# One product of two weight matrices in fp32 instead of split fp32r, and another rating of transfers in the planner

## The chip, the cores and the metric

The kernel runs on one core of one Trainium2 chip. The metric is the device time of one execution in microseconds (us); the kernel before was run three times, and its median counts.

## What is computed

Causal attention with a compressive memory, then two feed-forward blocks. The weights arrive as 8-byte floats (float64) and are converted on the chip.

```python
def _attn_ref(q, k, v, M_prev, z_prev, beta):      # B, H, S, D = 4, 8, 576, 64
    scores = scale * np.matmul(q, k.transpose(0, 1, 3, 2))
    ...                                            # causal mask, softmax
    local = np.matmul(a, v)
    q_p = phi(q)                                   # elu(q) + 1
    mem_out = einsum(q_p, M_prev) / (einsum(q_p, z_prev)[..., None] + 1e-06)
    g = 1.0 / (1.0 + np.exp(-beta))
    return g * mem_out + (1 - g) * local

def _moe_ref(x, w1, w2, w3, w_out):                # 2304 tokens, 512 wide, d_ff = 1024
    a = x @ w1
    b = x @ w2
    h = a * b @ w3
    return h @ w_out

def _moe2_ref(x, w_in, w_out):                     # d_ff = 2048
    h = x @ w_in
    g = h * np.tanh(softplus(h))
    return g @ w_out
```

## The kernel before

**The split.** A product of two fp32 matrices is mostly done as three fp32r products: each factor is split into a high part (a ScalarE cast to fp32r) and a low part (a VectorE subtraction of the high part from the value), and high x high, high x low and low x high are summed in PSUM (`HL`). The scores take two such products. The first twelve attention tasks (`T.f32`, `AVF=12`) multiply V with the exponentials, and M with PH, in plain fp32.

**w3 and w_out.** The first feed-forward block's last two factors are multiplied with each other once, ahead of everything that needs them: w3 @ w_out is 1024 x 512, computed as eight row blocks `f`. `load_wo(f)` brings a 128 x 512 block of w_out, `load_w3(f, hf)` a half of the transposed rows that belong to output block `f` (128 x 512), and `w3_mm(f, hf)` multiplies: for each of the eight 128-row blocks `c` of w_out three matmuls of 512 columns accumulate into one PSUM bank `w3p[f]`. After the second half the bank is split into wA buffers (L729 is the VectorE step), which ffn1 later uses as weights (`w3s`).

**Conversion.** `conv` loads a block of float64 (512 KB) into a raw buffer (`u`, `wE`, `wA`, or others), and builds an fp32 tile `c` from it: one ScalarE activation on the high words, one VectorE shift of the low words (L683), one VectorE shift-and-or that joins them (L685). `c` comes from the shared scratch tag `t`. `load_w` then splits `c` into a two-part fp32r tile: a cast (L337) and a subtraction (L333). Weights live in the tags `wA` (8 buffers), `wB` (8), `wD` (4), `wE` (4). w_out takes eight `wB`, each half block of w3 one `wD`. Later w1 and w2 go to `wE`, `wB` and `wD` (`fill_w12`), and the second feed-forward block's weights (`load_ffn2`) take whatever tags come free.

**Order.** Every operation is first recorded (`op`) with an engine, an estimated duration and the tiles that it reads and writes. `schedule` then simulates the engines with these estimates and fixes, for each engine, the order in which its instructions are issued; a buffer's next user waits until the last user of the buffer is done. Transfers are all issued by SyncE (SP), in the planner one after the other, each with the duration that `dma` states (250 bytes a ns, at least 500 ns), and behind it `LAT["sp"]` and `DMM`. TensorE's operations go by the order of recording, shifted by `GB` for the feed-forward work; the other engines go by the longest remaining chain. On the chip each engine runs its list in order, and waits where an input isn't there.

**The order of the work.** The loop over `heads` (two heads for each task; batch 0 is split into two halves of its rows) records for each step the scores of one head (`SC`), the AV product of the head before, the exponentials (`SE`), the memory product (`MEM`), and between them a share of the feed-forward work. In the first nine steps this share is w_out and w3: `start_w3` at step 0, `fill_w3` at the steps behind it, each with the two loads of block `f` and the product of block `f - 1`. w1 and w2 are loaded from step 6 on. After the eighth head the outputs X of batch 0's first half are there and ffn1 (`g<-x,wE` is its first product) begins. A task's output goes through transfers: the row sums (R) to memory `d`, back as `cp`, their reciprocals to memory again, and back broadcast as `Rr`, with which `mnl` is scaled and becomes `x`. ffn2 follows when all of ffn1 is done.

Of the kernel before, what the change touches and what calls it, by code (L numbers as in the profile page):

```python
# [8 lines left out]
F32 = mybir.dt.float32  # L9
F32R = mybir.dt.float32r  # L10
BF16 = mybir.dt.bfloat16
I32 = mybir.dt.int32
AF = mybir.ActivationFunctionType
ALU = mybir.AluOpType
P = 128
# [56 lines left out]
class Recorder:  # L72
# [9 lines left out]
    def op(self, eng, cost, fn, r=(), w=()):  # L82
        o = Op()
        o.eng, o.cost, o.fn, o.idx = eng, cost, fn, len(self.ops)
        o.deps, o.after, o.bufs, o.bias = set(), set(), [], self.bias
        for items, writing in ((r, False), (w, True)):
            for it in items:
                b, key = it if isinstance(it, tuple) else (it, None)
                if b not in o.bufs:
                    o.bufs.append(b)  # L90
                    if b.users:
                        o.after.add(b.users[0])
                    b.users.append(o)
                for k2, (ws, rs) in b.state.items():
                    if key is None or k2 is None or k2 == key:
                        o.deps.update(ws)
                        if writing:
                            o.deps.update(rs)
                if writing:
                    if key is None:  # L100
                        b.state.clear()
                    b.state[key] = ([o], [])
                else:
                    b.state.setdefault(key, ([], []))[1].append(o)
        o.deps.discard(o)
        o.after.discard(o)
        o.after -= o.deps
        self.ops.append(o)
        return o
# [136 lines left out]
def t_act(n, psum=False):  # L246
    return 0.833 * n + (51 if psum else 88)


def t_dve(n, fast=False):  # L250
    return (0.52 if fast else 1.042) * n + 68
# [6 lines left out]
def t_mm(n, m=128):  # L258
    return max(n * 0.433 + 7, m * 0.834)
# [3 lines left out]
def kernel(  # L263
# [15 lines left out]
    nc = tc.nc  # L279
    B, H, D, S = q.shape  # L280
    NT, DM = out.shape
    moe_w1, moe_w2, moe_w3, moe_w_out, moe2_w_in, moe2_w_out = (
        w.bitcast(I32) for w in (moe_w1, moe_w2, moe_w3, moe_w_out, moe2_w_in, moe2_w_out)
    )
# [12 lines left out]
    M1 = FF1 // P  # L297
    M2 = FF2 // P
    scale = 1.0 / float(D) ** 0.5

    rec = Recorder()
    op = rec.op
# [14 lines left out]
    def buf(tag, shape, dtype=F32):  # L317
        pool = wp if tag[0] == "w" else sp_
        return Buf(pool, shape, dtype, tag, BUFS[tag])
# [3 lines left out]
    def gbuf():  # L323
        return Buf(psG, [P, 512], F32, "g", 8)

    def dma(dst, src, nbytes, r=(), w=()):
        op("sp", max(500, nbytes / 250.0), lambda: nc.sync.dma_start(out=dst(), in_=src()), r, w)

    def mm(o, lhsT, rhs, start, stop):
        nc.tensor.matmul(out=o, lhsT=lhsT, rhs=rhs, start=start, stop=stop)  # L330
# [4 lines left out]
    def act(n, o, i, r, w, psum=False, func=AF.Copy, **kw):  # L335
        if func == AF.Copy:
            op("act", t_act(n, psum), lambda: nc.scalar.copy(out=o(), in_=i()), r, w)  # L337
        else:
            op("act", t_act(n, psum), lambda: nc.scalar.activation(out=o(), in_=i(), func=func, **kw), r, w)  # L339

    def lo(n, o, a, h, r, w, eng="dve"):
        e = nc.vector if eng == "dve" else nc.gpsimd
        op(eng, t_dve(n) if eng == "dve" else t_pool(n), lambda: sub(e, o(), a(), h().bitcast(F32)), r, w)
# [97 lines left out]
    def load_vm(T):  # L441
        j = T.nj
        n = 2 * j * DV
        if T.f32:
            M = T.M = buf("M", [P, VZ])
            dma(lambda: Vf.tile[:, T.i % 2, 0:j], lambda: v[T.b, T.p, :, 0:j], 512 * n, w=[(Vf, T.i % 2)])
            dma(lambda: M.tile, lambda: mz[T.b, T.p], 66560, w=[M])
            return
        raw = buf("vr", [P, VZ + 2 * NJ * DV])
        mr = lambda: raw.tile[:, 0:VZ]  # L450
        vr = lambda: raw.tile[:, VZ:VZ + n].rearrange("p (j t d) -> p j t d", t=2, d=DV)
        dma(vr, lambda: v[T.b, T.p, :, 0:j], 512 * n, w=[(raw, 0)])
        dma(mr, lambda: mz[T.b, T.p], 66560, w=[(raw, 1)])

        M = T.M = buf("M", [P, 2 * VZ], F32R)
        act(VZ, lambda: M.tile[:, 0:VZ], mr, [(raw, 1)], [(M, 0)])
        for a, b, c in ((0, P, VZ + 2), (P, VZ, VZ)):
            lo(b - a, lambda a=a, b=b, c=c: M.tile[:, c:c + b - a], lambda a=a, b=b: mr()[:, a:b], lambda a=a, b=b: M.tile[:, a:b], [(raw, 1), (M, 0)], [(M, 1)])
        act(n, lambda: Vb.tile[:, 0, 0:j], vr, [(raw, 0)], [(Vb, 0)])
        lo(n, lambda: Vb.tile[:, 1, 0:j], vr, lambda: Vb.tile[:, 0, 0:j], [(raw, 0), (Vb, 0)], [(Vb, 1)])  # L460
# [209 lines left out]

    def conv(src, rawb, c=None):
        raw = rawb()
        c = c or buf("t", [P, 512])
        flat = lambda: raw.tile.rearrange("p n w -> p (n w)")
        dma(flat, lambda: src, 524288, w=[raw])
        hw = lambda: raw.tile[:, :, 1]
        lw = lambda: raw.tile[:, :, 0]
        cv = lambda: c.tile  # L680
        ci = lambda: c.tile.bitcast(I32)
        act(512, cv, lambda: hw().bitcast(F32), [(raw, 1)], [c], False, AF.Prelu, scale=2.0 ** -111, alpha=-(2.0 ** 32))
        op("dve", t_dve(512, True), lambda: nc.vector.tensor_scalar(out=lw(), in0=lw(), scalar1=29, scalar2=None, op0=ALU.logical_shift_right),  # L683
           r=[(raw, 0)], w=[(raw, 0)])
        op("dve", t_dve(512), lambda: nc.vector.scalar_tensor_tensor(out=ci(), in0=ci(), scalar=3, in1=lw(), op0=ALU.logical_shift_left, op1=ALU.bitwise_or),  # L685
           r=[(raw, 0), c], w=[c])
        return c, cv

    def load_w(dst, src, m, tag, rawb, eng="dve"):
        c, cv = conv(src[m * P:(m + 1) * P, :], rawb)  # L690
        t = buf(tag, [P, 2, 512], F32R)
        act(512, lambda: t.tile[:, 0], cv, [c], [(t, 0)])
        lo(512, lambda: t.tile[:, 1], cv, lambda: t.tile[:, 0], [c, (t, 0)], [(t, 1)], eng)
        dst[m] = t
# [5 lines left out]
    w1s, w2s, w3s, wo, w3p, w3t = {}, {}, {}, {}, {}, {}  # L700

    def raw_u():
        return buf("u", [P, 512, 2], I32)

    def load_wo(f):
        load_w(wo, moe_w_out, f, "wB", lambda: buf("wA", [P, 512, 2], I32))

    def load_w3(f, hf):
        load_w(w3t, moe_w3, 2 * f + hf, "wD", lambda: buf("u" if hf or f > 5 else "wE", [P, 512, 2], I32))

    def w3_mm(f, hf):
        if hf == 0:
            w3p[f] = gbuf()
        ps = w3p[f]
        for c in range(4 * hf, 4 * hf + 4):

            def f2(c=c, t=w3t[2 * f + hf]):
                cs = slice((c - 4 * hf) * P, (c - 4 * hf + 1) * P)
                mm(ps.tile, t.tile[:, 0, cs], wo[c].tile[:, 0], c == 0, False)
                mm(ps.tile, t.tile[:, 0, cs], wo[c].tile[:, 1], False, False)  # L720
                mm(ps.tile, t.tile[:, 1, cs], wo[c].tile[:, 0], False, c == M1 - 1)

            t = w3t[2 * f + hf]
            op("pe", 3 * t_mm(512), f2, r=[(t, 0), (t, 1), (wo[c], 0), (wo[c], 1)], w=[ps])
        if hf == 0:
            return
        t = buf("wA", [P, 2, 512], F32R)
        act(512, lambda: t.tile[:, 0], lambda: ps.tile, [ps], [(t, 0)], True, AF.Identity, scale=2.0 ** -16)
        op("dve", t_dve(512), lambda: nc.vector.scalar_tensor_tensor(  # L729
            out=t.tile[:, 1], in0=ps.tile, scalar=2.0 ** -16, in1=t.tile[:, 0].bitcast(F32), op0=ALU.mult, op1=ALU.subtract),  # L730
           r=[ps, (t, 0)], w=[(t, 1)])
        w3s[f] = t
# [144 lines left out]
    def fill_w3(f):  # L877
        if f < M1:
            for hf in range(2):
                load_w3(f, hf)  # L880
        if f > CFG["W3G"]:
            w3_mm(f - 1, 0)
            w3_mm(f - 1, 1)

    def start_w3(hf):
        for f in range(4 * hf, 4 * hf + 4):
            load_wo(f)
        for f in range(CFG["W3G"]):
            load_w3(f, hf)
            w3_mm(f, hf)  # L890
# [15 lines left out]
    for i in range(NH_ + 1):  # L906
        if i < NH_:
            T, t = heads[i]
# [61 lines left out]
    for c in range(len(CH)):  # L970
        t0, n = CH[c]
        acc = []
        for t in range(n // P):
            x = gbuf()
# [69 lines left out]
```

## Time and profile before

| | |
|---|---|
| time, median of 3 runs | 989.56 us (988.12 to 990.38) |
| the profiled execution | 990.06 us, of which the span 988.3 us |
| TensorE busy | 948.4 us, 96% |
| VectorE busy | 742.1 us, 75% |
| ScalarE busy | 620.8 us, 63% |
| GpSimd busy | 82.6 us, 8% |
| moved by DMA | 96.63 MB, mean 98 GB/s |

The span runs from the first instruction to the last; the execution's time includes what lies around it. Matmuls are pipelined, so the time from one start to the next says what one costs, and a single record's duration is longer than that. PE is TensorE, PEld its weight loads, DVE VectorE, ACT ScalarE, POOL GpSimd, SP SyncE. The granted clock is a share of 2.4 GHz.

### The profile page before, as it was taken

To read this page: it belongs to the slowest core of one execution; us is meant where nothing else is said; L and a number is where in the kernel's file an instruction comes from. 1 tells how busy PE (TensorE), PEld (TensorE's weight loads), DVE (VectorE), ACT (ScalarE), POOL (GpSimd) and SP (SyncE) were. 2 spreads that over 40 slices of the span, in tenths; PEclk is the share of its full clock that TensorE was granted. 3 is DMA by queue.
4 is the path that set the end of the run, shared out by engine and by line. 5 is a ranking of instruction groups with operands and counts; after the bars stand their busy time and mean duration, and the time that the engine had idled before them with its cause. 6 is when DMAs were issued, how large, how long until landed. Compare 5 with 4: busy or idle time off the path is not lost.

```text
span 988.3 us, 15417 instructions
## 1 busy us (share of the span) xinstructions
PE 948.4 (96%) x5504; PEld 827.4 (84%) x5504; DVE 742.1 (75%) x1667; ACT 620.8 (63%) x1264; POOL 82.6 (8%) x70
## 2 busy tenths in 40 slices
PE   5897898999999999999999999999999999999998
PEld 3475796768999999999999998888888888998997
DVE  7899899999999898988562779665554756566663
ACT  5666587778988777866452667545444644555553
POOL 1111002221221111211000000000000000000000
PEclk7798799999999999999999999999999999999999
DMA  9436766643343332312471570011002000100000
GB/s 353 153 115 214 239 194 185 184 137 112 117 142 105 111 121 65 103 45 61 112 230 63 161 254 6 1 43 43 0 1 80 1 1 17 59 1 17 33 0 33
DMA packets 48317, 96.63 MB, mean 98 GB/s; under 512 B 11024, under 2 KB 23344, under 8 KB 48240
## 3 DMA queue, kind: packets, MB, share of 16 engines
q1 hardware_dynamic: 48240, 95.64, 30.7%
q8 instruction: 43, 0.70, 0.3%
q14 instruction: 34, 0.28, 0.1%
HBM read 85.85 MB, written 9.77 MB: 97 GB/s over the span
## 4 chain that ended last, share of the span: by engine, by line
PE 74%; DVE 15%; ACT 6%; issue 3%; DMA 2%; POOL 0%; SPq 0%; DVEq 0%; ACTq 0%; POOLq 0%
PE g L330 74%; DVE t L347 3%; DVE QK L333 3%; DVE e L347 2%; DVE t L685 1%; DVE mnl L347 1%; ACT t L339 1%; ACT e L339 1%; DVE g L560 1%; DVE u L333 1%; ACT mnl L337 1%; ACT t L337 1%; DVE wD L333 1%; DMA x2d<-t 0%; ACT QK L337 0%
## 5 line engine op out<-in xcount | busy, mean ns | idle before, releaser
L330 PE MATMUL g<-u,wA 128*128 128x288 f32 (+2 forms) x1008 | 163.0, 314 | 0.1
L330 PEld LDWEIGHTS g<-u,wA 128*128 128x128 f32 x1008 | 147.4, 188 | 8.9 <-DVE u L333 0.6
L347 DVE TENSOR_TENSOR t<-g,t 128x320 f32<-128x320 f32 (+6 forms) x344 | 122.5, 381 | 22.9 <-PE g L330 12.4
L580 POOL PARTITION_ALL_REDUCE t<-t x64 | 81.9, 1280 | 380.1 <-DVE t L347 310.7
L330 PE MATMUL g<-x,wB 128*128 128x288 f32 x768 | 111.0, 298 | 0.0
L330 PEld LDWEIGHTS g<-x,wB 128*128 128x128 f32 x768 | 104.9, 188 | 1.6 <-DVE t L347 0.7
L339 ACT ACTIVATE x<-x,two 128x512 f32<-128x512 f32 (+1 forms) x80 | 54.3, 681 | 68.9 <-DVE x L827 68.9
L330 PE MATMUL g<-e,V 128*65 128x320 f32 (+12 forms) x576 | 91.9, 306 | 4.6 <-ACT e L339 3.9
L339 ACT ACTIVATE x<-g 128x512 f32<-128x512 f32 (+1 forms) x98 | 55.0, 561 | 63.3 <-PE g L330 61.9
L330 PEld LDWEIGHTS g<-e,V 128*65 128x65 f32 (+1 forms) x576 | 67.2, 138 | 22.8 <-ACT e L339 6.6
L830 DVE SCALAR_TENSOR_TENSOR x<-g,x 128x512 f32<-128x512 f32 (+1 forms) x80 | 50.9, 638 | 42.0 <-ACT x L339 41.6
L330 PE MATMUL g<-QK 128*128 128x320 f32 (+7 forms) x464 | 72.7, 299 | 8.0 <-DVE QK L333 5.7
L330 PEld LDWEIGHTS g<-QK 128*128 128x128 f32 x464 | 64.9, 196 | 16.5 <-DVE QK L333 8.6
L337 ACT CAST x<-x 128x512 fp32r<-128x512 f32 (+1 forms) x80 | 46.1, 577 | 51.6 <-DVE x L347 51.4
L826 DVE TENSOR_SCALAR x<-x 128x512 f32<-128x512 f32 (+1 forms) x80 | 31.8, 398 | 61.7 <-ACT x L339 60.0
L330 PE MATMUL g<-wB,wD 128*128 128x512 f32 x192 | 58.7, 454 | 17.3 <-ACT wD L337 14.4
L333 DVE TENSOR_TENSOR t<-x 128x512 fp32r<-128x512 f32 (+1 forms) x80 | 50.9, 637 | 30.9 <-ACT x L337 29.6
L330 PEld LDWEIGHTS g<-wB,wD 128*128 128x128 f32 x192 | 39.3, 215 | 32.3 <-ACT wD L337 15.9
L333 DVE TENSOR_TENSOR QK<-ld,QK 64x640 fp32r<-64x640 f32 (+1 forms) x80 | 60.2, 753 | 2.8 <-ACT QK L337 1.3
L330 PE MATMUL g<-x,wE 128*128 128x288 f32 x384 | 55.5, 299 | 2.5 <-DVE e L347 1.9
L330 PE MATMUL g<-x,wD 128*128 128x288 f32 x384 | 57.0, 297 | 0.5 <-ACT t L339 0.5
L337 ACT COPY t<-g 128x288 f32<-128x288 f32 (+2 forms) x96 | 36.4, 393 | 32.4 <-PE g L330 26.3
(145 smaller groups left out, 1882.2 us busy)
## 6 DMA issues: line engine op xcount, KB each, us to landing
ld<-in_qk_dram SPq DMA_DIRECT2D x24, 608.0 KB
u<-in_moe_w_dram SPq DMA_DIRECT2D x26, 512.0 KB
Rr<-d SPq DMA_DIRECT2D x24, 288.0 KB
mnl<-in_moe_w_out_dram SPq DMA_DIRECT2D x11, 512.0 KB
mnl<-in_moe_w_in_dram SPq DMA_DIRECT2D x11, 512.0 KB
x2d<-t SPq DMA_DIRECT2D x16, 288.0 KB
out_dram<-x SPq DMA_DIRECT2D x18, 256.0 KB
wA<-in_moe_w_out_dram SPq DMA_DIRECT2D x8, 512.0 KB
```

The lines of the kernel that those rows point to most:

```text
L330: nc.tensor.matmul(out=o, lhsT=lhsT, rhs=rhs, start=start, stop=stop)
L333: eng.tensor_tensor(out=o, in0=a, in1=b, op=ALU.subtract)
L337: op("act", t_act(n, psum), lambda: nc.scalar.copy(out=o(), in_=i()), r, w)
L339: op("act", t_act(n, psum), lambda: nc.scalar.activation(out=o(), in_=i(), func=func, **kw), r, w)
L347: op(eng, t_dve(n) if eng == "dve" else t_pool(n), lambda: e.tensor_tensor(out=o(), in0=a(), in1=b(), op=alu), r, w)
L560: nc.vector.tensor_tensor(out=o, in0=o, in1=mv, op=ALU.add)
L580: op("pool", 430 + 2.6 * (b - a), lambda mv=mv: nc.gpsimd.partition_all_reduce(mv(), mv(), P, bass_isa.ReduceOp.max), r=[(m, x)], w=[(m, x)])
L685: op("dve", t_dve(512), lambda: nc.vector.scalar_tensor_tensor(out=ci(), in0=ci(), scalar=3, in1=lw(), op0=ALU.logical_shift_left, op1=ALU ...
L826: op("dve", t_dve(n, True), lambda: nc.vector.tensor_scalar(out=w_(), in0=u(), scalar1=E20, scalar2=2.0, op0=ALU.min, op1=ALU.add), r=[ub_ ...
L830: op("dve", t_dve(n), lambda: nc.vector.scalar_tensor_tensor(out=u(), in0=hv(), scalar=2.0 ** -8, in1=u(), op0=ALU.mult, op1=ALU.mult), r= ...
```

## The change

`conv` gets a parameter `part`: the fp32 value can be written into one part of a tile that the caller gives. `load_wo` and `load_w3` no longer split: they convert straight into fp32 tiles of two parts, two blocks of w_out to a `wB` tile, both halves of a block of w3 to a `wD` tile. `w3_mm` issues one fp32 matmul in place of three fp32r matmuls. The dependencies name the part. The planner's estimate for a transfer goes from 250 to 340 bytes a ns, for all transfers of the kernel, and that for a product of w3_mm to the fp32 rate.

```diff
--- before.py
+++ after.py
@@ -324,7 +324,7 @@
         return Buf(psG, [P, 512], F32, "g", 8)
 
     def dma(dst, src, nbytes, r=(), w=()):
-        op("sp", max(500, nbytes / 250.0), lambda: nc.sync.dma_start(out=dst(), in_=src()), r, w)
+        op("sp", max(500, nbytes / 340.0), lambda: nc.sync.dma_start(out=dst(), in_=src()), r, w)
 
     def mm(o, lhsT, rhs, start, stop):
         nc.tensor.matmul(out=o, lhsT=lhsT, rhs=rhs, start=start, stop=stop)
@@ -670,20 +670,21 @@
 
 
 
-    def conv(src, rawb, c=None):
+    def conv(src, rawb, c=None, part=None):
         raw = rawb()
         c = c or buf("t", [P, 512])
+        ck = (c, part)
         flat = lambda: raw.tile.rearrange("p n w -> p (n w)")
         dma(flat, lambda: src, 524288, w=[raw])
         hw = lambda: raw.tile[:, :, 1]
         lw = lambda: raw.tile[:, :, 0]
-        cv = lambda: c.tile
-        ci = lambda: c.tile.bitcast(I32)
-        act(512, cv, lambda: hw().bitcast(F32), [(raw, 1)], [c], False, AF.Prelu, scale=2.0 ** -111, alpha=-(2.0 ** 32))
+        cv = (lambda: c.tile) if part is None else (lambda: c.tile[:, part])
+        ci = lambda: cv().bitcast(I32)
+        act(512, cv, lambda: hw().bitcast(F32), [(raw, 1)], [ck], False, AF.Prelu, scale=2.0 ** -111, alpha=-(2.0 ** 32))
         op("dve", t_dve(512, True), lambda: nc.vector.tensor_scalar(out=lw(), in0=lw(), scalar1=29, scalar2=None, op0=ALU.logical_shift_right),
            r=[(raw, 0)], w=[(raw, 0)])
         op("dve", t_dve(512), lambda: nc.vector.scalar_tensor_tensor(out=ci(), in0=ci(), scalar=3, in1=lw(), op0=ALU.logical_shift_left, op1=ALU.bitwise_or),
-           r=[(raw, 0), c], w=[c])
+           r=[(raw, 0), ck], w=[ck])
         return c, cv
 
     def load_w(dst, src, m, tag, rawb, eng="dve"):
@@ -702,26 +703,28 @@
     def raw_u():
         return buf("u", [P, 512, 2], I32)
 
+
     def load_wo(f):
-        load_w(wo, moe_w_out, f, "wB", lambda: buf("wA", [P, 512, 2], I32))
+        if f % 2 == 0:
+            wo[f] = wo[f + 1] = buf("wB", [P, 2, 512])
+        conv(moe_w_out[f * P:(f + 1) * P, :], lambda: buf("wA", [P, 512, 2], I32), wo[f], f % 2)
 
     def load_w3(f, hf):
-        load_w(w3t, moe_w3, 2 * f + hf, "wD", lambda: buf("u" if hf or f > 5 else "wE", [P, 512, 2], I32))
+        if hf == 0:
+            w3t[f] = buf("wD", [P, 2, 512])
+        x = 2 * f + hf
+        conv(moe_w3[x * P:(x + 1) * P, :], lambda: buf("u" if hf or f > 5 else "wE", [P, 512, 2], I32), w3t[f], hf)
 
     def w3_mm(f, hf):
         if hf == 0:
             w3p[f] = gbuf()
-        ps = w3p[f]
+        ps, t = w3p[f], w3t[f]
         for c in range(4 * hf, 4 * hf + 4):
 
-            def f2(c=c, t=w3t[2 * f + hf]):
-                cs = slice((c - 4 * hf) * P, (c - 4 * hf + 1) * P)
-                mm(ps.tile, t.tile[:, 0, cs], wo[c].tile[:, 0], c == 0, False)
-                mm(ps.tile, t.tile[:, 0, cs], wo[c].tile[:, 1], False, False)
-                mm(ps.tile, t.tile[:, 1, cs], wo[c].tile[:, 0], False, c == M1 - 1)
-
-            t = w3t[2 * f + hf]
-            op("pe", 3 * t_mm(512), f2, r=[(t, 0), (t, 1), (wo[c], 0), (wo[c], 1)], w=[ps])
+            def f2(c=c, t=t):
+                mm(ps.tile, t.tile[:, hf, (c - 4 * hf) * P:(c - 4 * hf + 1) * P], wo[c].tile[:, c % 2], c == 0, c == M1 - 1)
+
+            op("pe", 2 * 0.833 * 512 + 4, f2, r=[(t, hf), (wo[c], c % 2)], w=[ps])
         if hf == 0:
             return
         t = buf("wA", [P, 2, 512], F32R)
```

## Rows read from the trace of the kernel before

**Rows 1.** The profile's page: TensorE's line of the busy times, and the granted clock over 40 equal slices of the span, in tenths.

```profile
PE 948.4 (96%) x5504; PEld 827.4 (84%) x5504; DVE 742.1 (75%) x1667; ACT 620.8 (63%) x1264; POOL 82.6 (8%) x70
...
PEclk7798799999999999999999999999999999999999
```

**Rows 2.** Windows over the whole span: the stretch in us, its length, the busy time of each engine with its instructions, TensorE's mean granted clock, the busy share of the DMA engines, GB/s.

```profile
5.00:15.00 10.00, 5.75 (x17) 3.73 (x18) 7.84 (x23) 5.86 (x12) 1.42 (x2) 0.94 1.02 404
...
95.00:103.60 8.60, 2.38 (x4) 0.59 (x4) 6.42 (x13) 4.68 (x10) 0.00 (x0) 0.54 0.93 278
...
113.00:150.00 37.00, 37.00 (x263) 34.39 (x263) 35.41 (x87) 29.87 (x67) 3.17 (x3) 1.00 0.62 199
150.00:250.00 100.00, 92.27 (x569) 72.18 (x568) 94.47 (x264) 77.89 (x174) 25.52 (x21) 1.00 0.50 147
250.00:300.00 50.00, 48.64 (x365) 46.12 (x364) 49.18 (x123) 44.33 (x99) 10.83 (x8) 1.00 0.43 128
...
400.00:988.00 588.00, 584.04 (x3217) 518.03 (x3216) 377.03 (x730) 319.08 (x608) 12.76 (x10) 1.00 0.18 57
```

**Rows 3.** The same view, with the first 113 us cut in three. The columns are those of PE, PEld, DVE, ACT and POOL, then the clock, the DMA share and GB/s.

```profile
0.00:37.00 37.00, 22.59 (x60) 13.04 (x61) 29.93 (x82) 22.96 (x43) 4.58 (x9) 0.78 0.72 272
37.00:83.00 46.00, 44.71 (x204) 32.50 (x204) 39.42 (x100) 30.20 (x64) 6.72 (x5) 0.96 0.51 161
83.00:113.00 30.00, 19.57 (x68) 14.08 (x67) 25.01 (x56) 18.17 (x37) 1.65 (x1) 0.72 0.75 236
```

**Rows 4.** The view of waits, from 0 to 113 us: who waited for whom, us in total, times, the longest.

```profile
PE g L330 <- ACT wD L337: 14.4, 5, 5.5
...
ACT wB L337 <- DVE t L685: 7.4, 7, 1.5
```

**Rows 5.** The timeline of TensorE: start in us, us until the end of the last of the group, and in brackets the idle time before it with what ended it. g<-wB,wD is the product of w3 and w_out, g<-x,wE the first of ffn1.

```profile
63.71 7.78 PE L330 MATMUL g<-wB,wD 128*128 128x512 f32 x33
71.33 1.14 PE L330 MATMUL g<-QK 128*128 128x288 f32 x6
...
103.65 8.40 PE L330 MATMUL g<-wB,wD 128*128 128x512 f32 x24 [5.49 <-ACT wD L337]
...
113.12 1.75 PE L330 MATMUL g<-x,wE 128*128 128x288 f32 x12
```

**Rows 6.** VectorE: two rows of the groups by line with the shapes apart, from 0 to 113 us (busy us, mean ns of one, idle before), and two of its timeline, one subtraction and what starts next.

```profile
L333 DVE TENSOR_TENSOR wD<-t,wD 128x512 fp32r<-128x512 f32 x16 | 11.5, 716 | 2.9 <-ACT wD L337 2.9
...
L333 DVE TENSOR_TENSOR wB<-t,wB 128x512 fp32r<-128x512 f32 x9 | 6.2, 690 | 1.6 <-ACT wB L337 1.6
...
45.12 0.68 DVE L333 TENSOR_TENSOR wD<-t,wD 128x512 fp32r<-128x512 f32 x1
45.72 0.78 DVE L347 TENSOR_TENSOR e<-g,t 128x288 f32<-128x288 f32 x3
```

**Rows 7.** The instructions on the tiles of wB over the whole span: ScalarE's casts (shortest, median and longest in ns, first and last start in us).

```profile
L337 ACT CAST wB<-t x24: 602/620/625, 11.6 to 569.2; 128x512 fp32r<-128x512 f32 x24
```

**Rows 8.** Products in plain fp32: the matmuls on the tile M over the whole span with their forms (those with 2 output rows are issued by the fp32 tasks alone), and lines of TensorE's timeline.

```profile
L330 PE MATMUL g<-PH,M x144: 289/299/847, 6.8 to 455.1; 128*128 128x288 f32 x80, 128*2 128x288 f32 x32, 128*4 128x288 f32 x32
...
165.92 0.65 PE L330 MATMUL g<-PH,M 128*128 128x288 f32 x2
166.40 1.25 PE L330 MATMUL g<-e,V 128*65 128x288 f32 x6
...
181.03 1.23 PE L330 MATMUL g<-PH,M 128*128 128x288 f32 x4
182.18 1.05 PE L330 MATMUL g<-u,wA 128*128 128x288 f32 x6
```

**Rows 9.** The waits of SyncE's queue, which issues the transfers, from 20 to 65 us.

```profile
SPq L327 <- DVE cp L653: 12.6, 1, 12.6
SPq L327 <- DVE PH L498: 12.0, 1, 12.0
```

**Rows 10.** Timelines of TensorE, SyncE and VectorE: the output of the fourth task from its last AV product to x, and (the first two lines) one transfer of Rr of an earlier task with the VectorE step that uses it.

```profile
75.16 1.25 SPq L327 DMA_DIRECT2D Rr<-d  x2
...
79.67 0.75 DVE L347 TENSOR_TENSOR mnl<-mnl,Rr 128x576 f32<-128x576 f32 x1
...
82.66 1.01 PE L330 MATMUL g<-e,V 128*65 128x288 f32 x6
...
84.68 0.52 SPq L327 DMA_DIRECT2D d<-R  x1
...
86.79 0.33 SPq L327 DMA_DIRECT2D cp<-d  x1
...
92.10 0.23 DVE L653 TENSOR_SCALAR cp<-cp,eps 128x9 f32<-128x9 f32 x1
...
93.76 0.33 SPq L327 DMA_DIRECT2D d<-cp  x1
...
96.16 1.23 SPq L327 DMA_DIRECT2D Rr<-d  x2
...
104.84 0.75 DVE L347 TENSOR_TENSOR mnl<-mnl,Rr 128x576 f32<-128x576 f32 x1
...
107.56 0.46 DVE L333 TENSOR_TENSOR x<-mnl,x 128x288 fp32r<-128x288 f32 x1
```

## The prediction

> **What bounds the kernel now.** I read the page's busy shares first: TensorE is busy 96% of the span and its granted clock is full except in some of the first five slices [rows 1]. That says where to look, not what is to be had. So next the windows. From 113 us on TensorE is nearly always busy: all of 113 to 150, 92.27 of 100 us in 150 to 250, 48.64 of 50, and 584.04 of 588 us after 400. VectorE is full beside it until 300 us (35.41 of 37, 94.47 of 100, 49.18 of 50) [rows 2]. Before 113 us, the stretch in which w3 and w_out are converted and multiplied, TensorE is busy 22.59 of 37, 44.71 of 46 and 19.57 of 30 us, at a granted clock of 0.78, 0.96 and 0.72 [rows 3]. Busy time times clock is 17.6 + 42.9 + 14.1 = 74.6 us of work at full clock in 113 us. The other 38.4 us are 26.1 us of idle time and 12.3 us lost to the clock, which stands at 0.54 in the emptiest piece [rows 2]; a 0.54 is nearly all at the lower level, 1.2 GHz. The loss is at both ends of the stretch, not in its middle.
>
> The waits say who causes it: TensorE waits 14.4 us for the ScalarE cast of w3 into wD, and ScalarE's cast into wB waits 7.4 us for the VectorE step before it [rows 4]. The timeline of TensorE shows the last wait at its place: the product of the last block of w3 starts at 103.65 us after 5.49 us idle, and at 113.12 us the first product of ffn1 follows it [rows 5]. So in the first stretch the conversion of weights decides at its ends, TensorE in its middle.
>
> **Part 1: casts and subtractions go.** Eight blocks of w_out and sixteen of w3 each lose one ScalarE cast and one VectorE subtraction. The profile before has 16 subtractions into wD in this stretch, and nine into wB, of which eight are w_out's [rows 6]. One lasts 0.69 us, but the next instruction starts 0.60 us after it (45.12 to 45.72) [rows 6], so 24 of them are 14.4 us of VectorE, out of 29.93 + 39.42 + 25.01 = 94.4 us that it is busy in the stretch [rows 3]. The casts are 24 x 0.62 us = 14.9 us of ScalarE [rows 7]; it is busy 71.3 of 113 us [rows 3], so they count only by the latency of one cast and one subtraction, some 1.3 us, at each place where TensorE waits.
>
> **Part 2: TensorE gets dearer.** Of three fp32r products of 512 columns one fp32 product is left, 64 in place of 192. The old price: 33 of them start at 63.71 us and the next thing starts at 71.33, so 0.231 us each and 0.693 us for three [rows 5]. This trace has no fp32 product of 512 columns, but the attention's first twelve tasks multiply PH and M in fp32. The two-column form is issued 16 times by them (eight half tasks, four whole ones with two halves) and has 32 records [rows 8], so one fp32 product runs as two passes. One such product of 288 columns takes from 165.92 to 166.40, 0.48 us [rows 8], which makes 0.48 x 512/288 = 0.853 us for 512 columns. The dearest clean reading is four passes from 181.03 to 182.18, 0.2875 us a pass [rows 8], hence 1.02 us. A gain is excluded, since two passes at 0.24 us for 288 columns can't undercut three at 0.231 us for 512. So 64 products cost 64 x 0.16 = +10.2 us at full clock, at most 64 x 0.33 = +21 us. I take the lower price, since the second reading changes its weights between full and two-column forms and includes a wait.
>
> The Trainium skill, in "FP8 and Floating Point Precision", TensorE Precision Notes, says that true fp32 takes four passes through the array. That speaks against the change: at 0.231 us a pass it would be 0.924 us for each product and 14.8 us in all, and the forecast would be some 3 us later. The trace shows two records for each product, at 0.24 us for 288 columns, so it agrees only if each record holds two passes; the measured duration is what I sum.
>
> **Part 3: buffers.** w_out takes four of the eight buffers of wB in place of eight, so four blocks of w1 and w2 can be converted before the last w3 product gives w_out free; now the first of them has to wait for that. A buffer of wD holds a whole block of rows, so w3 may run four blocks ahead in place of two. The 24 conversions also stop using the shared scratch buffers. None of this adds an instruction; I cost it at nothing, up to 2 us gained after 113 us because those conversions leave a stretch where VectorE is full.
>
> **Part 4: the rating.** The program orders each engine's instructions ahead of time with estimated durations, in which transfers run one after the other. By the windows the stretch moves 272 x 37 + 161 x 46 + 236 x 30 ns = 24.6 MB [rows 3], which the planner counts as 98 us at 250 bytes a ns and 72 us at 340. The chip reached 404 GB/s from 5 to 15 us [rows 2]. So the old plan held the transfer queue to be nearly full and placed the conversions late in VectorE's order. On the chip the queue stands behind such placements: 12.0 us for an instruction on PH and 12.6 us for one on cp [rows 9], with the loads of w3 queued behind. The new plan should place both earlier. The danger is the other side: a step planned too early stalls everything behind it on VectorE, and the order of the whole kernel changes, transfers after the first stretch too. I bound this at 3 us either way after 113 us and take 0.
>
> **The sum, by stretch.** 0 to 37 us: ten of the subtractions lie here, 10 x 0.60 = 6.0 us of a VectorE busy 29.93 of 37 us; the product of w3's first block follows the last conversion. Against it 8 x 0.16 us, doubled at the low clock, at most 2.6 us. The last of w_out's loads is hardly the limit, as the transfers are dense until 25 us only. I take -5 us (between 0, if waits take the place of the subtractions, and -8, if the new plan also brings the last conversions forward).
>
> 37 to 83 us: 44.71 of 46 us busy [rows 3], so the dearer products lie on the path: five of the eight blocks, 40 x 0.16 = +6.4 us; from the 1.3 us of idle time and the lost clock little comes back. +6 us (+5 to +13, with the upper price).
>
> 83 to 113 us: TensorE has only 14.1 us of work at full clock here, 16.7 with the dearer products. VectorE has 20 fewer subtractions behind it, 12 us in which it can convert ahead, and the last product needs no cast and subtraction. What is late next is the attention output of the fourth task, which ffn1 needs: its AV product starts at 82.66 and its x is ready at 107.56 + 0.46 = 108.0 us [rows 10]. Its steps without waiting in VectorE's order: 2.0 us to the first d, 2.1 to cp, 2.1 again for cp to land (taken as the step before), 1.7 for VectorE until d is written back, 2.4 until Rr is issued, at most 4.5 us for Rr (75.16 to 79.67), and 3.2 from mnl to x [rows 10]: 18 us. So x is at 83 + 18 = 101 us, and the stretch can end some 21 us after 83 in place of 30: -9 us (-4 to -12).
>
> After 113: nothing in the sum but -1 us for part 3 (-3 to +3). Together -5 + 6 - 9 - 1 = -9 us. The profiled execution has 988.3 us of span and took 990.06 us, 1.8 us around it; it lies 0.5 us above the median of the three runs, 989.56. So 990.06 - 9 = 981.0 us.
>
> **Rivals.** (a) TensorE takes it all: the stretch is bound by TensorE from 37 us to its end, because the last products (16 x 0.16 us more, up to double at the low clock) run back to back behind a middle that is 6 to 13 us longer, and the ends give back little. This decides if the first product of w3 still ends after 34 us and the fourth task's chain still takes over 23 us. Its price is +10.2 us less 3 us of casts: 997 us. For it speaks the full middle; against it the 38.4 us that TensorE now loses. Chance 0.15.
>
> (b) The saving is hidden: the chain from the last AV product to x [rows 10], four transfers and their places in VectorE's order, stays at 25 us, so that only the start gains and the middle takes it back: -5 + 6 = about 990 us. For it speaks that x comes at 108.0 us, 5 us before ffn1, already now; against it that 7 us of that chain are spent waiting in VectorE's order. Chance 0.12.
>
> (c) More than forecast: the new plan also removes the queue's two long stalls, and TensorE is limited by its work alone. 74.6 + 10.2 = 84.8 us of work, behind a first 10 us in which it can't be full, lets ffn1 start at about 95 us: -18 us, 972 us. Chance 0.18.
>
> **How the numbers follow.** The forecast with its neighbourhood (976 to 986) has 0.55. The range takes in (c) and the upper fp32 price with a weak start, and leaves out the worse half of (a): 969 to 994 us. A measurement of this kernel can tell some 0.2%, 2 us, from no change. Faster by more than that: 0.55 + 0.18 and a little of (b), 0.75. Within it: most of (b), 0.10. Slower: 0.15.
>
> **What would show it.** In the profile after: 128 TensorE records of wB with wD, with 0.85 us from one product to the next (1.02 would prove the upper price); no cast or subtraction into wD or wB from w3 and w_out; the first block's product over by about 32 us; the middle stretch some 6 us longer; the first ffn1 product at 100 to 106 us; and from there to the end the same 875 us as now. I am wrong if ffn1 starts after 111 us, or if it starts early and the stretch after it grows by what was won, which would lay the blame on the new order.

## The result and the profile after

The changed kernel takes 965.42 us (median of four runs, 964.73 to 968.32), the kernel before 989.39 us: a ratio of 0.9765 (95% interval 0.9747 to 0.9783), 24 us less. The forecast was 981.0 us with a range of 969 to 994. The direction was right, the size was not, and the time lies 3.6 us below the range.

The page of the profile after, the lines that answer to [rows 1] and the group of the products:

```profile
span 964.1 us, 15222 instructions
...
PE 945.7 (98%) x5440; PEld 808.9 (84%) x5440; DVE 725.8 (75%) x1643; ACT 607.0 (63%) x1240; POOL 86.4 (9%) x70
...
PEclk9999999999999999999999999999999999999999
...
L330 PE MATMUL g<-wB,wD 128*128 128x512 f32 x128 | 61.6, 619 | 3.9 <-DVE wD L686 2.1
```

The span is TensorE's busy time plus its idle time. Busy went from 948.4 to 945.7 us, idle from 39.9 to 18.4. That the busy time fell although the products got dearer is the clock: it is granted in full from the first slice to the last now, so the 12 us that the low clock cost before are gone, and about as much dearer work has taken their place.

The windows, to be set against [rows 2] and [rows 3] (length, then the busy times of PE, PEld, DVE, ACT and POOL, the clock, the DMA share, GB/s):

```profile
0.00:37.00 37.00, 27.04 (x89) 13.99 (x90) 31.27 (x90) 23.18 (x44) 6.31 (x10) 1.00 0.90 331
37.00:83.00 46.00, 46.00 (x148) 22.63 (x148) 42.97 (x115) 32.36 (x69) 6.75 (x5) 1.00 0.74 224
83.00:113.00 30.00, 29.49 (x160) 21.54 (x159) 29.64 (x68) 24.96 (x54) 2.63 (x2) 1.00 0.87 290
```

```profile
113.00:150.00 37.00, 36.46 (x240) 30.56 (x239) 36.49 (x101) 26.45 (x61) 6.93 (x5) 1.00 0.46 147
150.00:250.00 100.00, 98.63 (x645) 82.24 (x644) 92.79 (x251) 80.20 (x181) 26.35 (x20) 1.00 0.46 135
```

In the first 113 us TensorE is now busy 102.5 us (86.9 before) and VectorE 103.9 us (94.4 before), although 24 subtractions are gone: both engines have taken in work that came later before. From 150 to 250 us TensorE's idle time went from 7.7 to 1.4 us.

TensorE's timeline shows what was moved:

```profile
26.77 1.13 PE L330 MATMUL g<-wB,wD 128*128 128x512 f32 x2 [0.18 <-DVE wB L686]
...
63.88 1.01 PE L330 MATMUL g<-e,V 128*65 128x288 f32 x6
64.73 8.83 PE L330 MATMUL g<-wB,wD 128*128 128x512 f32 x20
73.39 1.23 PE L330 MATMUL g<-PH,M 128*128 128x288 f32 x4
74.55 7.99 PE L330 MATMUL g<-wB,wD 128*128 128x512 f32 x18
82.22 1.78 PE L330 MATMUL g<-QK 128*128 128x288 f32 x10
83.84 1.88 PE L330 MATMUL g<-wB,wD 128*128 128x512 f32 x4
...
87.87 7.89 PE L330 MATMUL g<-wB,wD 128*128 128x512 f32 x18
95.19 3.77 PE L330 MATMUL g<-x,wE 128*128 128x288 f32 x24
```

The first block's products end at 26.77 + 1.13 = 27.9 us. In the kernel before, the same view has their end at 34.93 + 1.95 = 36.9 us:

```profile
34.93 1.95 PE L330 MATMUL g<-wB,wD 128*128 128x512 f32 x3 [0.39 <-ACT wB L337]
```

The eighth AV product of the attention comes at 63.88 us, before at 82.66 [rows 10]. Behind it lie 60 of the 128 passes of w3 and w_out (20, 18, 4 and 18), 30 of the 64 products; before, the last two blocks, 16 products, lay there. Part of them are done while the fourth task's output goes its way through memory: its x is written from 87.74 us on (the line below, of VectorE's timeline), before from 107.56, when 42 of the 60 passes are through. ffn1 starts behind the last 18 at 95.19, before at 113.12 [rows 5], with no idle time ahead of it. 20 passes from 64.73 to 73.39 us are 0.433 us a pass, 0.866 us a product.

```profile
87.74 0.45 DVE L333 TENSOR_TENSOR x<-mnl,x 128x288 fp32r<-128x288 f32 x1
```

By stretch, against the sum: to the end of the first block -9.0 us (forecast -5), from there to ffn1 76.2 to 67.3, so -8.9 us (forecast +6 - 9 = -3), after the start of ffn1 875.2 to 868.9, so -6.3 us (forecast -1). Together -24.2 us of span.

### The profile page after: what moved, and what is told of

Read it like the earlier page. It is cut to its first block, busy times and chain, and to the rows that moved or that the text cites. A ratio compares the mean times of both kernels' runs of the same rounds, so it can differ in the third digit from the quotient of the medians.

```text
span 964.1 us, 15222 instructions
## 1 busy us (share of the span) xinstructions
PE 945.7 (98%) x5440; PEld 808.9 (84%) x5440; DVE 725.8 (75%) x1643; ACT 607.0 (63%) x1240; POOL 86.4 (9%) x70
## 3 DMA queue, kind: packets, MB, share of 16 engines
q1 hardware_dynamic: 48240, 95.64, 31.3%
## 4 chain that ended last, share of the span: by engine, by line
PE 67%; DVE 18%; ACT 6%; DMA 4%; issue 3%; SPq 1%; POOL 0%; DVEq 0%; ACTq 0%; POOLq 0%
PE g L330 67%; DVE t L347 4%; DVE QK L333 3%; DMA Rr<-d 2%; DVE e L333 1%; DVE e L347 1%; ACT t L339 1%; DVE mnl L347 1%; DVE g L560 1%; SPq L327 1%; DVE u L333 1%; DVE t L686 1%; ACT mnl L337 1%; DMA wA<-in_moe_w_out_dram 1%; ACT R L337 1%
## 5 line engine op out<-in xcount | busy, mean ns | idle before, releaser
L347 DVE TENSOR_TENSOR t<-g,t 128x288 f32<-128x288 f32 (+6 forms) x344 | 121.3, 380 | 22.2 <-PE g L330 14.4
L580 POOL PARTITION_ALL_REDUCE t<-t x64 | 85.8, 1342 | 352.0 <-DVE t L347 282.5
L330 PE MATMUL g<-wB,wD 128*128 128x512 f32 x128 | 61.6, 619 | 3.9 <-DVE wD L686 2.1
L347 DVE TENSOR_TENSOR x<-x 128x512 f32<-128x512 f32 (+1 forms) x80 | 51.0, 637 | 6.0
```

The lines of the kernel that those rows point to most:

```text
L347: op(eng, t_dve(n) if eng == "dve" else t_pool(n), lambda: e.tensor_tensor(out=o(), in0=a(), in1=b(), op=alu), r, w)
L580: op("pool", 430 + 2.6 * (b - a), lambda mv=mv: nc.gpsimd.partition_all_reduce(mv(), mv(), P, bass_isa.ReduceOp.max), r=[(m, x)], w=[(m, x)])
```

## The experiments

Theory A is that of the prediction: the casts and subtractions that went are the gain, the rating is worth nothing. Theory B is its rival: the rating is the gain, through another order. Every run was timed beside the kernel before (989.1 to 989.6 us); a ratio's interval is at 95%.

**One part at a time.** The rating alone, on the kernel before:

```diff
-        op("sp", max(500, nbytes / 250.0), ...
+        op("sp", max(500, nbytes / 340.0), ...
```

> The kernel before with the rating of 340 bytes a ns alone; the products stay split in fp32r. Theory A (the casts and subtractions that went are the gain): the 14.4 us of VectorE are still there, so 985 to 990 us, first ffn1 product not before 109 us. Theory B (the rating is the gain, by another order): 966 to 972 us, first ffn1 product at 95 to 99 us. If both count, between.

Measured: 979.90 us, ratio 0.9906 (0.9889 to 0.9922). The other part alone, the changed kernel with the old rating:

```diff
-        op("sp", max(500, nbytes / 340.0), ...
+        op("sp", max(500, nbytes / 250.0), ...
```

> The changed kernel with the old rating of 250 bytes a ns: fp32 products, packed buffers, no casts and subtractions. Theory A: 965 to 971 us. Theory B: 985 us or later, since the loads and conversions are planned as late as before. A theory C, that the fp32 products keep the granted clock up by their length, expects a clock of 0.98 or more in the first 113 us here, and 0.9 or less in the run with the rating alone.

Measured: 979.88 us, ratio 0.9914 (0.9898 to 0.9930). Neither theory holds alone: each part is worth some 9 us by itself, and the rating is worth 14.5 us beside the fp32 products. Each of these is the time of one order; how far it can be trusted is shown below. Theory C fails: in the first 113 us the clock is 0.92 with fp32 products and the old rating, 0.95 with fp32r and the new one.

The old rating leaves the late wait in place. This is TensorE's timeline of fp32_r250; the last 16 passes wait for a conversion into wD, as in [rows 5], with 5.53 us of idle time (L686 is the step that was L685):

```profile
24.77 6.66 PE L330 MATMUL g<-wB,wD 128*128 128x512 f32 x8 [2.30 <-DVE wD L686]
...
70.55 1.01 PE L330 MATMUL g<-e,V 128*65 128x288 f32 x6
...
93.22 9.93 PE L330 MATMUL g<-wB,wD 128*128 128x512 f32 x16 [5.53 <-DVE wD L686]
102.58 2.16 PE L330 MATMUL g<-x,wE 128*128 128x288 f32 x12
```

The chain that ends in this wait (from 86.66 to 93.08 us) runs through steps of ScalarE and VectorE on wA, t, wE and wD, one behind the other, and through no transfer: the conversion stands late in their order. The old rating also keeps the long stall of the transfer queue. By the view of waits up to 100 us it stands 12.3 us behind VectorE's step on cp, as in [rows 9]; that wait ends at 52.20 us, and what it alone costs is not shown.

```profile
SPq L327 <- DVE cp L653: 18.3, 3, 12.3
```

In the changed kernel, the same view has no wait of the queue longer than 5.9 us:

```profile
SPq L327 <- DVE t L686: 9.5, 6, 2.5
SPq L327 <- DVE QK L333: 8.5, 4, 5.9
...
SPq L327 <- DVE cp L653: 3.0, 1, 3.0
```

With the rating alone (r340_only), VectorE is as full as after, 104.0 of the first 113 us, but has the 24 subtractions to do in them. ffn1 starts only 1.9 us later than after, and its first products wait for x:

```profile
97.09 1.36 PE L330 MATMUL g<-x,wE 128*128 128x288 f32 x9
99.17 0.40 PE L330 MATMUL g<-x,wE 128*128 128x288 f32 x1 [0.72 <-ACT x L337]
100.28 5.33 PE L330 MATMUL g<-x,wE 128*128 128x288 f32 x38 [0.71 <-DVE x L333]
```

These two waits are 1.4 us. Most of the distance to the changed kernel comes later: from ffn1's start to the end it takes 881.8 us, the changed kernel 868.9.

**The buffers.** Packing undone, the rest as changed:

```diff
-        if f % 2 == 0:
-            wo[f] = wo[f + 1] = buf("wB", [P, 2, 512])
-        conv(..., wo[f], f % 2)
+        wo[f] = buf("wB", [P, 2, 512])
+        conv(..., wo[f], 0)
...
+        w3t[x] = buf("wD", [P, 2, 512])
+        conv(..., w3t[x], 0)
...
```

> The changed kernel with one block of w_out to a wB tile and one half block of w3 to a wD tile again (half of each tile unused). If the freed buffers are part of the gain, w1 and w2 are converted later and w3 runs only two blocks ahead: 970 to 976 us. If they count for nothing: 965 us within 2.

Measured: 969.83 us, ratio 0.9805 (0.9791 to 0.9820), 4.4 us above the changed kernel. The next experiments say how far such a difference can be trusted.

**The rating's size.** Only the number differs:

> The changed kernel with 400 bytes a ns in the plan, the rate that the trace shows from 5 to 25 us. If the gain of the rating is its nearness to what the chip does, another 1 to 3 us less: 962 to 965 us. If it is the luck of one order among many: anywhere from 960 to 975 us.

> The changed kernel with 300 bytes a ns in the plan. Between 250 (979.9 us) and 340 (965.4 us) if time follows the rating smoothly: 969 to 974 us. If each rating is one draw among orders, it may lie outside of these two: below 964 or above 981 us.

> The changed kernel with 320 bytes a ns in the plan. Smooth between 300 (970.4 us) and 340 (965.4 us): 966 to 970 us. One draw among orders: anywhere from 962 to 976 us.

> The changed kernel with 360 bytes a ns in the plan. Smooth between 340 (965.4 us) and 400 (972.7 us): 966 to 970 us. One draw among orders: anywhere from 962 to 976 us.

And the rating for the loads of weights alone (`dma(..., rate=340.0)` in conv, 250 elsewhere):

> The changed kernel with 340 bytes a ns in the plan for the loads of weights alone, 250 for all others. If the rating helps because the plan held the queue to be full of weights in the first stretch: 964 to 968 us. If the other transfers' places count (row sums, K and Q): 975 to 982 us.

Then the rating held fixed, and the order changed by something that means next to nothing, `DMM=850` for `DMM=800`:

> The changed kernel at its own 340 bytes a ns, with the planner's margin behind a transfer at 850 in place of 800 ns: a change that means next to nothing by itself and gives another order. If 965.4 us is a lucky order among those that the new rating can give: 967 to 975 us, as with 300, 320, 360 and 400. If 340 itself is right: 964 to 967 us.

> The same margin at the old rating of 250 bytes a ns, with the fp32 products. If the old rating is bad by its size: 976 to 984 us, near the 979.9 us of the margin of 800. If that too was a draw: it may fall to 966 to 975 us.

| bytes a ns | margin 800 | margin 850 |
|---|---|---|
| 250 | 979.88 us | 982.52 us |
| 300 | 970.35 us | |
| 320 | 971.06 us | |
| 340 | 965.42 us (the change) | 972.69 us |
| 340, weights alone | 973.10 us | |
| 360 | 974.21 us | |
| 400 | 972.68 us | |

The six orders with 300 and more for all transfers have a mean of 971.1 us and lie between 965.4 and 974.2, without a trend; both with 250 lie at 980 to 983. So the rating's size is worth about 10 us (981.2, the mean of two orders, less 971.1), and the changed kernel is the best draw of six, some 6 us better than their mean. The traces show the same two groups: the queue's longest wait up to 100 us is 12.3 and 12.4 us with 250, at most 7.7 us with 300 and more, and ffn1 starts at 102.6 and 102.1 us with 250, between 95.2 and 98.9 with the others. The 4.4 us of the packing and the 7.7 us between all transfers and the weights alone are no larger than what a draw makes, and say nothing sure.

**What the stretch hangs on, with the order kept.** From here the planner's estimates are untouched, so each engine runs the order of the changed kernel, and only what an instruction takes is changed. More work first. One more VectorE subtraction behind each of the 24 conversions:

```diff
+            if part is not None:
+                sub(nc.vector, lw().bitcast(F32), cv(), cv())
```

> The changed kernel with 24 subtractions more on VectorE, one behind each conversion of a block of w3 or w_out, whose result nobody reads; nothing is planned for them, so the orders stay. They take what the removed ones took, 24 x 0.6 = 14.4 us, but no product waits for them. If VectorE's work sets the end of the first stretch (theory A in its strong form): 976 to 981 us. If the gain came from the shorter chain of cast and subtraction ahead of the products, or from the order alone: 965 to 968 us.

Measured: 982.05 us, ratio 0.9927 (0.9912 to 0.9942), so +16.6 us. The forecast price was 14.4 us; by the windows VectorE is busy 102.5 us up to ffn1's start, 86.2 in the changed kernel, so the added work took some 16.3 us. ffn1 starts at 110.9 us, 15.7 later. The products of two blocks issued twice:

```diff
+                if f in (3, 4):
+                    mm(ps.tile, a, b, c == 0, False)
+                    mm(ps.tile, a, b, False, c == M1 - 1)
...
+        sc = 2.0 ** (-17 if f in (3, 4) else -16)
```

> The changed kernel with the fp32 products of blocks 3 and 4 of w3 issued twice (the sum is halved behind it), 16 products of 0.866 us = 13.9 us more on TensorE, the order kept. If TensorE too has no room from 37 to 95 us, as its busy share says: 978 to 981 us. If VectorE alone binds and TensorE's full busy share only hides its waiting: 966 to 970 us.

Measured: 980.72 us, ratio 0.9911 (0.9896 to 0.9926), +15.3 us for 13.9 us. ffn1 starts at 108.5 us, 13.3 later. The start of ffn1 is read from these rows on the tiles of wE, of dve24 and pe_twice:

```profile
L330 PE MATMUL g<-x,wE x384: 291/297/696, 110.9 to 543.1; 128*128 128x288 f32 x192
...
L330 PE MATMUL g<-x,wE x384: 291/297/695, 108.5 to 541.3; 128*128 128x288 f32 x192
```

Added work on either engine is paid in full, and nearly all of it before ffn1. Now less work. Six of eight products on a quarter of the columns:

```diff
+                n = 512 if c in (0, M1 - 1) else 128
+                mm(ps.tile[:, 0:n], ..., wo[c].tile[:, c % 2, 0:n], ...)
```

> The changed kernel, the same order of all instructions, but six of the eight products of each block of w3 with w_out take only 128 of the 512 columns (the rest of their sum is left out). 48 products become some 0.65 us shorter, 31 us in all. If TensorE binds the stretch before ffn1, as its 100% busy share from 37 us on says, most of it comes back: 935 to 945 us. If VectorE or the loads stand right behind it, less than 10 us: 956 to 965 us.

Measured: 973.54 us (969.39 to 975.41), ratio 0.9839 (0.9812 to 0.9865): with some 31 us less work on TensorE, by the price of a product, the kernel is 8 us slower. Its windows from 65 to 83 us, a line of its timeline that answers to the one at 73.39 us after, and two from ffn1's start on:

```profile
65.00:83.00 18.00, 13.90 (x51) 8.20 (x49) 17.43 (x45) 12.99 (x28) 1.18 (x1) 0.74 0.92 275
```

```profile
75.06 2.38 PE L330 MATMUL g<-PH,M 128*128 128x288 f32 x4 [3.82 <-DVE PH L498]
...
93.13 3.77 PE L330 MATMUL g<-x,wE 128*128 128x288 f32 x24
100.42 1.03 PE L330 MATMUL g<-e,V 128*65 128x288 f32 x4 [3.52 <-ACT e L339]
```

TensorE now waits 3.82 us for VectorE, the granted clock of the piece is 0.74, and the next products take 2.38 us in place of 1.23. Up to ffn1's start TensorE is busy 67.1 us (85.0 in the changed kernel), of which the clock of 0.89 costs about 7.4 us, and idle 26.0 us (10.2). So ffn1 does start earlier, at 93.13 us, but only by 2.1 us. VectorE is busy 52.5 of the 56.1 us from 37 us to that start. What makes this kernel slower than the changed one lies behind it: from ffn1's start to the end it takes 874.5 us in place of 868.9, and one part of that is the wait of 3.52 us for the exponentials. The profile is that of the fastest of the four runs (969.39 us); where the others lose more is not shown. Without the low parts of w1 and w2 (the 16 subtractions go, the products read the high part in their place), and both reliefs together:

```diff
-        lo(512, lambda: t.tile[:, 1], cv, ...)
+        if eng == "none":
+            op("dve", t_dve(512), lambda: None, [c, (t, 0)], [(t, 1)])
+        else:
+            lo(512, lambda: t.tile[:, 1], cv, ...)
...
-                        mm(..., wcol(w, wi, kk), ...)
+                        mm(..., wcol(w, 0, kk), ...)
```

> The changed kernel without the 16 VectorE subtractions that make the low parts of w1 and w2; the products read the high part in their place, as many and as long as before, and the order of all the rest stays. 16 x 0.6 = 9.6 us less on VectorE, nearly all between 65 and 135 us. If VectorE alone binds there: 955 to 958 us. If TensorE binds there beside it: 962 to 965 us.

> The same without the 16 subtractions, and with six of eight products of w3 with w_out on 128 of 512 columns: both engines relieved. If both bind together, so that neither alone gives time back, this is much faster than either: 945 to 955 us. If something else sets the end (loads, the chain of attention, the clock that falls when TensorE waits): 962 to 973 us.

Measured: 966.70 us (965.90 to 967.26) and 968.23 us (966.65 to 970.08). The first is a weak test of VectorE before ffn1: only eight of the 16 subtractions lie ahead of ffn1's start in the changed kernel, and VectorE's busy time up to it falls from 86.2 to 83.2 us. Then the loads, the bytes of w1 and w2 halved, and all three reliefs at once:

```diff
+    def conv_half(src, rawb):
...
+        op("sp", 524288 / 340.0, lambda: nc.sync.dma_start(out=raw.tile[:, 0:256, :]..., in_=src[:, 0:512]), [], [raw])
...
-        c, cv = conv(...)
+        c, cv = (conv_half if src is moe_w1 or src is moe_w2 else conv)(...)
```

> The changed kernel with loads of w1 and w2 of half their bytes (the first half of each block is read twice by the conversion; the VectorE shift is half as long, 16 x 0.13 us; the rest and its order stay): 16 x 256 KB less between 50 and 115 us, where the DMA engines are 93 to 97% busy from 65 to 95 us. If the loads alone set the end there: 958 to 962 us. If they are one of several: 963 to 966 us.

> The same half loads together with both reliefs before (no low parts of w1 and w2, short products of w3): TensorE, VectorE and the DMA engines have all less to do before 115 us. If the three bind together: 945 to 958 us. If the chain of attention (scores, maximum, exponentials, AV, row sums and back) in the planned order sets the end: 963 to 969 us again.

Measured: 964.87 us (964.69 to 965.77) and 965.83 us (963.91 to 969.26). With everything light, no engine is quite full, and ffn1 starts at 92.62 us, 2.6 earlier; the windows of all_light:

```profile
37.00:83.00 46.00, 36.66 (x150) 23.20 (x150) 41.01 (x112) 33.33 (x72) 6.72 (x5) 0.81 0.64 195
83.00:113.00 30.00, 26.39 (x167) 21.80 (x168) 25.58 (x67) 26.81 (x58) 2.60 (x2) 1.00 0.71 225
```

So in this order neither TensorE's work alone nor the loads of w1 and w2 set the end from below: relief turns into waiting, and the clock is 0.81 from 37 to 83 us. VectorE is not ruled out: of its 86.2 busy us up to ffn1 79.0 are left here, and from 37 to 83 us it is still busy 41.01 of 46 us.

**Work moved to GpSimd.** The 16 subtractions of w1 and w2 given to GpSimd, in the plan too:

```diff
-        load_w(w1s, moe_w1, m, ..., raw_u)
+        load_w(w1s, moe_w1, m, ..., raw_u, "pool")
...
```

> The changed kernel with the 16 subtractions that split w1 and w2 on GpSimd in place of VectorE, planned at GpSimd's price (1.25 us each). If VectorE's work sets the end: up to 9.6 us less, 956 to 961 us. If not, 965 us, or later by GpSimd's slower subtraction ahead of ffn1's first products: 966 to 972 us.

Measured: 1012.80 us, ratio 1.0231 (1.0211 to 1.0251), 47 us above the changed kernel. One of GpSimd's groups, three of the waits (60 to 220 us), then two lines of TensorE's timeline:

```profile
L333 POOL TENSOR_TENSOR wB<-t,wB 128x512 fp32r<-128x512 f32 x8 | 11.6, 1454 | 16.9 <-ACT wB L337 9.9 <-ACT t L339 7.0
```

```profile
DVE e L347 <- POOL t L580: 19.6, 4, 8.8
...
POOL t L580 <- issue: 19.2, 3, 6.6
...
POOL wB L333 <- ACT wB L337: 9.9, 3, 5.3
```

```profile
132.09 3.70 PE L330 MATMUL g<-e,V 128*65 128x288 f32 x10 [5.20 <-ACT e L339]
148.09 4.00 PE L330 MATMUL g<-e,V 128*65 128x288 f32 x10 [7.38 <-ACT e L339]
```

VectorE waits 19.6 us for the attention's maximum (L580), and TensorE up to 7.38 us for the exponentials. Waiting for the casts is not what holds the maximum up. In this window it follows a subtraction on GpSimd three times, and each time 6.2 to 6.6 us lie between the end of the subtraction and its start, 19.2 us in all, for which the profile shows nothing that it waits for ("issue"); these make up nearly all of VectorE's wait. What GpSimd does in that time the profile doesn't show. By the windows ffn1 starts 12.7 us later than in the changed kernel (107.89), and in the 112 us behind it TensorE is idle 17.5 us in place of 1.3. The order of the whole kernel is another one too, so how much of the 47 us is GpSimd's own is open.

## Why the prediction was wrong

**The step that failed is part 4.** "I bound this at 3 us either way after 113 us and take 0": the rating was worth 9.3 us alone and 14.5 us beside the fp32 products. The mechanism stood in the part, conversions placed late in VectorE's order and the queue behind its late steps on PH and cp, and the price was left at nothing. About 10 us of it go with the size of the rating, as the table shows; the rest, some 5 us, is the draw of one order, which no profile of the kernel before could show. How the 10 us divide between the queue's stalls and the late conversions was not tried.

**Parts 1 to 3 held as a sum, not in their terms.** Without the rating the kernel takes 979.88 us, 9.3 us less than before, and 982.52 us in the second order; the sum had -9. By the first one's profile (span 980.8 us) the first block ends at 24.77 + 6.66 = 31.4 us, -5.5 (forecast -5), from there to ffn1 it is 71.2 us, -5.0 (forecast -3), and after ffn1's start 878.2 us, +3.0 (forecast -1). That the middle figure is near is luck: from the first block to the eighth AV product (70.55 us) it is 6.7 us less than before, where the sum had +6, and from there to ffn1 1.6 us more, where it had -9.

**The price of a product was right**: 0.866 us, forecast 0.853 (upper end 1.02). The sum of work came near: up to ffn1's start TensorE is idle 10.2 us by its windows, at a granted clock of 1.00, so it is busy 95.2 - 10.2 = 85.0 us; rival (c) had 84.8. It is not quite the same work, since 146 passes of the attention lie before ffn1 now and 136 did before.

**That the dearer products lie on the path in the middle was wrong.** "+6 us" supposed that five blocks stay between the heads of the attention. In the new order the eighth AV product is 18.8 us earlier, 26 products and not 40 lie between the first block and it, and that piece is 9.8 us shorter. The -9 us behind it were wrong too: from the eighth AV product to x it takes 24.3 us (25.4 before, forecast 18), and to ffn1 31.3 us (30.5 before), because 30 products stand there in place of 16. Rival (c) named this end, TensorE limited by its work alone, and put ffn1 at "about 95 us" (it was 95.2); it had 972 us and a chance of 0.18. The further 6.3 us came after ffn1's start, where TensorE's idle time fell; the sum allowed 3.

**Rivals (a) and (b)** did not come as times: the stretch did not get longer, and x comes 19.8 us earlier. But what they said of the chain was right, it still takes over 23 us; it starts earlier.

**Left open**: which chain sets the end of the first stretch in the new order. Added work on VectorE or TensorE is paid in full, while much less work on TensorE, up to 7.2 us less on VectorE and half the loads of w1 and w2 bring ffn1 at most 2.6 us forward and give nothing in the end. That VectorE's remaining work sets the end is a rival that no run rules out. That waiting and the lower clock take back what lighter products give is read from the windows, and was not tried by itself. The share of the packed buffers can't be told from a draw.

## What to carry to other kernels

An estimate in a planner that orders in-order queues is a change of every queue: price it by the stalls that the queue shows now, not at nothing; and try several orders that differ in nothing that matters before a few us are given a cause. A busy share of 100% says that more work will be paid, not that less will be given back; only a run with less work, in the same order, says that. And a sum that comes out right may hold two wrong terms: check a forecast piece by piece.

## What was not expected of the hardware

With 17.9 us less busy time on TensorE, ffn1 started only 2.1 us earlier: TensorE was idle 15.9 us more, its granted clock was 0.74 between 65 and 83 us where it had been 1.00, and the same four passes took 2.38 us in place of 1.23. A subtraction of 128x512 took 1.45 us on GpSimd (planned at 1.25), 0.69 us on VectorE [rows 6]. Between a subtraction on GpSimd and the maximum behind it lay 6.2 to 6.6 us in which the profile shows no wait.
